# Four layers of attention, forward and backward: packed scores in layer 3, more transposes by DMA, and edits around them

## The chip, the core and the metric

The kernel runs on one core of a Trainium2 chip. The core has four compute engines with an instruction stream each: TensorE (PE, matmuls and transposes; its weight loads are listed as PEld), VectorE (DVE), ScalarE (ACT) and GpSimd (POOL). SyncE (SP) issues the DMAs, which run on 16 DMA engines. The metric is the device time of one execution in microseconds (us), and less is better.

## What is computed

Four residual layers over x of 2048 rows and 640 columns with 32 heads of 20: A, B, A, B, and then the gradients with respect to x and the four weights. The kernel numbers the layers 0 to 3: 0 and 2 are of kind A, 1 and 3 of kind B.

```python
def _A_ref(x, wqkv, wo):                    # linear attention
    ...
    phi = lambda t: jnp.where(t > 0, t + 1, jnp.exp(t)) + 1e-6
    pq, pk = phi(q), phi(k)
    kv = jnp.einsum("bhsd,bhse->bhde", pk, v)
    z = jnp.einsum("bhsd->bhd", pk)
    num = jnp.einsum("bhqd,bhde->bhqe", pq, kv)
    den = jnp.einsum("bhqd,bhd->bhq", pq, z)[..., None] + 1e-6
    ...
def _B_ref(x, wqkv, wo):                    # sliding window of 256
    ...
    scores = jnp.einsum("bhqd,bhkd->bhqk", q, k) * (Dh ** -0.5)
    mask = (idx[:, None] - idx[None, :] >= 0) & (idx[:, None] - idx[None, :] < W)
    p = _softmax(jnp.where(mask[None, None], scores, -1e9), axis=-1)
    o = jnp.einsum("bhqk,bhkd->bhqd", p, v)
    ...
x = x + _A_ref(_layernorm(x), A_wqkv, A_wo)
x = x + _B_ref(_layernorm(x), B_wqkv, B_wo)
x = x + _A_ref(_layernorm(x), A_wqkv, A_wo)
x = x + _B_ref(_layernorm(x), B_wqkv, B_wo)
_out, _vjp = jax.vjp(_f, A_x, A_wqkv, A_wo, B_wqkv, B_wo)
```

With tiles of 128 rows, a tile of queries meets three tiles of keys in a B layer: the first is half masked by the window (a key k counts for a query q of the tile if k > q), the middle one is full, and the last one is half masked by causality (k <= q).

## The kernel before

Rows are worked in 16 tiles of 128, heads in 8 groups of four. The order on PE, DVE, ACT and POOL is the order in which the program issues instructions. That order is written out by hand: the table PLACES (L41) holds due times, in slots, for the pieces of a tile's or a chunk's work, and `slots` (L737) sorts the pieces into the steps of the loop that carries the stage. SP's DMAs are all on one queue and start in the order of issue.

The stages follow each other. The forward of layer 0 is first. Then come 128 steps of layer 1, in which layer 0's rear and layer 2's front also run, and 128 steps of layer 3 with layer 2's rear. Next is the backward of layer 3, called a core: 8 chunks of two query tiles, 32 steps a chunk. The backward of linear layer 2 and the core of layer 1 follow. Last are the backward of layer 0 and the weight gradients, whose matmuls fill what PE has left (`fill`, L1298).

A forward step (`run`, L334) takes one query tile and one group. `f_scores` (L361) issues up to 12 matmuls: for each of the three key tiles one for each of four heads, which lie on four row groups of PE. Their output sT is one PSUM tile, with one buffer (L301). One exp on ACT (L376) turns all its columns, 128 for each key tile and head, into eT, which comes from a pool of five (L250). Then the due pieces of the plan are issued. After them `f_masks` (L379) zeroes the halves on POOL with two selects (L382 the diagonal, L386 the first key tile), and `b_pv` (L211) multiplies the eT of two steps before with the values, for each head and key tile. A backward core needs Wo transposed; for layer 3 a transposing DMA loads it near the end of the forward (L322, `turned`, L148).

A core step (`core_step`, L631) makes scores s and the products dp for a pair of heads, exp of s on ACT (L653), and ds = dp times e on DVE (L656). It transposes the ds of four steps before, either on PE with a copy by ACT or DVE (L676, L681, L683) or, where `by_dma` (L623) says so, with a transposing DMA that is issued as soon as ds is made. The table `bd` chooses these steps from step 64 on, `xx` shifts the copies between ACT and DVE, and warming transposes (`warm`, L168) are added where PE has little to do. The products (`core_acc`, L689) come `lag` = 7 steps behind the scores. Slabs of q, k and v are loaded a quarter of a chunk ahead.

`plan_before` (L743) prepares the gradient of the attention output for a chunk: g times Wo, the product with o summed over each head (`fold`, `split`, on POOL), and its transposes (`flip8`). For layer 1's first chunk it runs ahead of the core, inside the last slots of layer 2's backward (L1265 to L1267). `plan_linear` (L916) is the backward of a linear layer, in 8 slots a tile. Its `part` (L938) makes the gradient dqa: PE's product times fd, the derivative of phi, which is min(phi - 1e-6, 1) (L957 to L960).

Of the kernel before, what the change touches and what calls it, by code (L numbers as in the profile page):

```python
# [11 lines left out]
ALU = mybir.AluOpType  # L12
# [5 lines left out]
H = 32  # L18
DH = 20
HP = 32  # L20
T = 2048
TT = T // P
DT = D // P
# [18 lines left out]
    f1=[0.1, 1.7, 2.5, 6.6, 9.6, 12, 13.2, 14.1, 14.5, 14.6, 14.5, 16.1],  # L42
    f2=[-27.5, -23.6, -21.5, -20.6, -19.5, -17.9, -16.5, -15.1, -13.5, -7.8, -6.9, -5.5, -4.7, -3.8, -2.9, 11, 12, 13, 14, 17.6, 22.4, 23.3, 24, 25.1, 26.4, 27.3],
    f3=[-35.7, -30, -26.5, -25, -24, -23.8, -22.5, -18, -16.4, -14, -12.1, -7.4, -6.8, -6, -4.9, -3.5, -1.7, 11.3, 12.4, 13.4],
    bf=[2.1, 3.1, 5.7, 15.4, 18.3, 6.2, 7.8, 10, 14.7, 29.2],
    bh=[13.1, 14.5, 15.5, 17.1, 17.5, 18, 20.5, 21.2, 25.7, 28.3, 30, 35, 19.1, 20, 21.8, 22.5, 23.3, 24.6, 25.2, 27.5, 30.5, 31.7, 33, 35, 41, 43, 2.2, 8.3, 9.5, 12, 18.9, 32],
    l2=[-12.1, -3.2, 0.6, 0.7, 2.3, 2.7, 4.7, 5.6, 6.5, 7, 5, 8, 8.3, 11.5, 11.8, 14, 14.6, 15.4, 16, 17.7, 19.4],
    n1=[10, 0.8, 3.3, 3.5, 3.8, 7, 3.6, 4.2, 5.5, 6.6, 8],
    xx=[1, 0, 0, 0, 0, 0, 0, 1, 1, 0, 1, 0, 0, 1, 0, 0, 0, 1, 0, 0, 0, 0, 1, 0, 0, 0, 0, 0, 0, 0, 1, 0],
    bd=[0, 0, 1, 0, 0, 0, 1, 0, 0, 0, 0, 0, 0, 0, 1, 0, 0, 0, 1, 0, 0, 0, 1, 0, 0, 0, 1, 0, 0, 0, 1, 0])  # L50


class Kern:
    def __init__(self, ctx, tc, x0, A_w, A_wo, B_w, B_wo, grad, outs):
        self.ctx, self.tc = ctx, tc
        self.nc = nc = tc.nc
        self.W = dict(A=A_w, B=B_w)
        self.Wo = dict(A=A_wo, B=B_wo)
        self.grad = grad
# [36 lines left out]
        self.r = [const.tile([P, TT, H], F32, name=f"r{l}") for l in range(4)]  # L96
        self.mz = {l: const.tile([KB, 6, KA], BF, name=f"mz{l}") for l in (0, 2)}
        self.mzT = {l: const.tile([KA, 6, KB], BF, name=f"mzT{l}") for l in (0, 2)}
        self.dmz = const.tile([KB, 6, KA], BF, name="dmz")
        self.dmzT = const.tile([KA, 6, KB], BF, name="dmzT")  # L100
        self.macc = const.tile([KB, 6, KA], F32, name="macc")
# [109 lines left out]
    def b_pv(self, st, l, t, g, e, nb, rings, o):  # L211
# [4 lines left out]
            st.first = None  # L216
        for hh in range(4):
            for i in range(nb):
                ins = self.mm(st.ops[:, 4 * q + hh, :], e[:, hh, i * P:(i + 1) * P],
                              rings[i]["s"][:, 2, 4 * g + hh, 0:HA], st.first is None, i == nb - 1)  # L220
                if st.first is None:
                    st.first = ins
                else:
                    self.after(ins, st.first)
# [10 lines left out]
    def forward(self, st):  # L235
# [11 lines left out]
        st.sm = self.pool(keep, "fm", 4, side="right")  # L247
        st.fa = self.pool(keep, "fa", 3, side="right")
        st.xm = self.pool(keep, "xm", 5, side="right")
        st.fpe = self.pool(keep, "pe", 5, side="right")  # L250
        wo = self.pool(keep, "wo", 1, side="right")
        rings = {i: self.pool(keep if i in (0, 3, 4) else early, f"ring{i}", 1, side="right") for i in (0, 3, 4, 1, 2)}
        st.fb = self.pool(early, "fb", 3, side="right")
# [64 lines left out]
        def begin_slabs():  # L318
            early.close()
            self.core_slabs(3, st.core)  # L320
            self.core_buffers(st, st.core)
        plan += [(END - 32, begin_core), (END - 31, lambda: self.turned(st.core.WoT, "B")), (END - 6, begin_slabs)]  # L322
        first_ = {}

        def before(a):
# [8 lines left out]
        def run(n):  # L334
            u, fs = None, slots[n]
            if B1 <= n < B1 + G * TT:
                if n == B1:
                    for f in fs:
                        f()
                    fs = []  # L340
                u = self.f_scores(st, *divmod(n - B1, G), X[1])
            elif B3 <= n < END:
                u = self.f_scores(st, *divmod(n - B3, G), X[3])
            for f in fs:
                f()
# [15 lines left out]
    def f_scores(self, st, t, g, X):  # L361
# [5 lines left out]
        rings = [st.ring[(k0 + i) % len(st.ring)] for i in range(nb)]  # L367
        qT = st.ring[t % len(st.ring)]["T"]
        s = st.pS.tile([P, 4, 512], F32, name="sT")
        for i in range(nb):  # L370
            for hh in range(4):
                r0 = HP * hh
                self.mm(s[:, hh, i * P:(i + 1) * P], rings[i]["T"][r0:r0 + HP, 1, g, :], qT[r0:r0 + HP, 0, g, :],
                        True, True, (r0, 0))
        e = st.fpe.tile([P, 4, 3 * P], BF, name="eT")
        nc.scalar.activation(e[:, :, 0:nb * P], s[:, :, 0:nb * P], ACT.Exp)  # L376
        return t, g, e, nb, rings, X[t]["ob"]

    def f_masks(self, t, g, e, nb, rings, o):  # L379
        nc = self.nc  # L380
        dg = e[:, :, (nb - 1) * P:nb * P]
        nc.gpsimd.affine_select(out=dg, in_=dg, compare_op=ALU.is_ge, fill=0.0, base=0,  # L382
                                pattern=[[0, 4], [1, P]], channel_multiplier=-1)
        if nb == 3:
            fr = e[:, :, 0:P]
            nc.gpsimd.affine_select(out=fr, in_=fr, compare_op=ALU.is_ge, fill=0.0, base=-1,  # L386
                                    pattern=[[0, 4], [-1, P]], channel_multiplier=1)

    def plan_ln(self, st, l, t, x, src, key, pool):

# [349 lines left out]
            out[int(at)].append(fn)  # L740
        return [(lambda fs=fs: [f() for f in fs]) if fs else None for fs in out]

    def plan_before(self, st, l, c, B, at=(PLACES["bf"][:5], PLACES["bf"][5:]), l0=0):  # L743

        nc = self.nc
        r = self.r[l]
# [6 lines left out]
        for i, (f0, p0, p1, sp, f8) in enumerate(at):  # L753
# [12 lines left out]
            def fold(i=i, t=t):  # L766
                R = B.ring[t % 4]
                pr = x["pr", i] = B.sf.tile([P, H, DH], F32, name="prod")
                nc.gpsimd.tensor_tensor(out=pr, in0=R["ds"][:, :, 0:DH], in1=self.heads(x["o"][:, i, :]), op=ALU.mult)
                for m in (DH // 2, DH // 4):  # L770
                    nc.gpsimd.tensor_tensor(out=pr[:, :, 0:m], in0=pr[:, :, 0:m], in1=pr[:, :, m:2 * m], op=ALU.add)

            def split(i=i, t=t):
                R = B.ring[t % 4]
                m = DH // 4
                ds, pr = R["ds"], x["pr", i][:, :, 0:m]
                nc.gpsimd.tensor_scalar(out=ds[:, :, DH:DH + m], in0=pr, scalar1=-1.0, scalar2=None, op0=ALU.mult)
                nc.gpsimd.tensor_tensor(out=ds[:, :, DH + m:DH + 2 * m], in0=pr, in1=ds[:, :, DH:DH + m], op=ALU.add)

            def flip8(t=t):  # L780
                R = B.ring[t % 4]
# [134 lines left out]
    def plan_linear(self, st, lp, l, t, X, WT, g_out):  # L916
# [21 lines left out]
        def part(nm, c):  # L938
# [15 lines left out]
            if nm == "pk":  # L954
                nc.scalar.copy(dst, ps[:, 0:CW])  # L955
            else:
                f = lp.le.tile([P, CW], F32, name="fd")  # L957
                nc.vector.tensor_scalar(out=f, in0=src("pq" if nm == "dn" else "pk")[:, c * CW:(c + 1) * CW], scalar1=-EPS, scalar2=1.0,
                                        op0=ALU.add, op1=ALU.min)
                nc.vector.tensor_tensor(out=dst, in0=ps[:, 0:CW], in1=f, op=ALU.mult)  # L960

        def turn_q():
# [248 lines left out]
    def passes(self):  # L1211
# [6 lines left out]
        with ExitStack() as rest:  # L1218
# [45 lines left out]
                self.core_slabs(1, B)  # L1264
            b0 = base + 8 * (TT - 1) + PLACES["n1"][0]  # L1265
            plan.append((b0, begin))
            plan += [(b0 + a, f) for a, f, *_ in self.plan_before(st, 1, 0, B, (PLACES["n1"][1:6], PLACES["n1"][6:11]), -10)]  # L1267
            for f in self.slots(plan, int(max(a for a, _ in plan)) + 1):
                if f is not None:
                    f()  # L1270
# [2 lines left out]
            st.ps = st.ps2  # L1273

            self.core_buffers(st, B)
            left1 = self.core(st, 1, self.gs[0], B, [])
            for f in left1[:8]:
                if f is not None:
                    f()
# [8 lines left out]
            W.ps = self.pool(rest, "wp", 2, bass.MemoryType.PSUM, "right")  # L1288
            wl = self.pool(rest, "wl", 2)
            W.rhs = self.pool(rest, "wq", 2)  # L1290
            wo = self.pool(rest, "wo", 3)
            st.ex = self.pool(psl, "ex", 1)
            W.lhs, W.tight = [wl, wl], True
            W.out = lambda: wo.tile([P, 240], BF, name="wr")
# [24 lines left out]
            with ExitStack() as es, ExitStack() as le:  # L1319
# [11 lines left out]
                for f in self.slots(plan, int(max(a for a, *_ in plan)) + 1):  # L1331
                    if f is not None:
                        f()
                    fill(0.6)
            wl4 = self.pool(rest, "wl", 2)
            W.lhs += [wl4, wl4, wl, wl3]
            W.tight = False
# [61 lines left out]
```

## Time and profile before

| what | us |
|---|---|
| median of three runs (2276.66 to 2277.54) | 2276.91 |
| the profiled execution | 2281.01 |
| its span, first to last instruction | 2279.3 |
| layer 3 forward, 431 to 695 us: PE / DVE / ACT / POOL busy of 264 | 238 / 173 / 194 / 159 |
| core of layer 3, 695 to 1110: of 415 | 386 / 325 / 322 / 281 |
| layer 2 backward, 1184 to 1306: of 122 | 106 / 100 / 73 / 43 |
| core of layer 1, 1322 to 1746: of 424 | 395 / 332 / 329 / 288 |
| weight gradients alone, 2036 to 2280: of 244 | 240 / 19 / 11 / 0 |

In the lines of the profile, times in groups are a mean in ns or a sum in us; a line of a timeline has its start, its duration, the engine, the line of the code, the operation with the tiles it writes and reads, and in brackets how long the engine had stood idle and what ended that. A line of the windows view has a stretch, its length, the busy time of PE, PEld, DVE, ACT and POOL with counts, the granted clock of TensorE (1.00 is full speed), the DMA engines' mean busy share and GB/s.

### The profile page before, as it was taken

The numbers are of one execution on the slowest core, as the hardware profiler recorded it, in microseconds if no ns is written. First come the engines' busy times: TensorE is split into PE (matmuls) and PEld (weight loads), VectorE is DVE, ScalarE is ACT, GpSimd is POOL, SyncE is SP. The second block draws the span as 40 slices with busy tenths as digits, with TensorE's granted clock in tenths as the row PEclk, the third lists the DMA queues.
The fourth block names the chain that finished last, engine by engine and source line by source line (L and its number), as shares of the span: only waits on it lengthen the run. The fifth ranks groups of instructions, "written<-read, shape, count | busy, mean of one in ns | idle before, by whom it ended". The sixth has DMA issues, their size and how long they took to land. (4 is left out here: it accounts for less than half of the span.)

```text
span 2279.3 us, 77671 instructions
## 1 busy us (share of the span) xinstructions
PE 2096.7 (92%) x32468; PEld 1711.2 (75%) x32468; DVE 1453.8 (64%) x2980; ACT 1365.5 (60%) x2125; POOL 1092.1 (48%) x1892
## 2 busy tenths in 40 slices
PE   7889998899989999999878889999998898999999
PEld 5667776577767877777757768777777697889999
DVE  6778885777734788888748858888877244520000
ACT  5467887377766878878736668788876243430000
POOL 2046665166665577777533456777775312220000
PEclk9899999999989999999989999999999999999999
DMA  7488875698888577776488743777764999875753
GB/s 253 141 232 229 225 222 148 162 226 213 215 223 219 144 162 186 184 181 170 116 285 238 197 114 88 176 183 181 181 168 116 290 279 279 245 211 156 181 147 89
DMA packets 666992, 436.20 MB, mean 191 GB/s; under 512 B 406928, under 2 KB 643472, under 8 KB 666256
## 3 DMA queue, kind: packets, MB, share of 16 engines
q1 hardware_dynamic: 666640, 431.24, 71.4%
q8 instruction: 254, 4.16, 0.8%
q14 instruction: 98, 0.80, 0.1%
HBM read 213.09 MB, written 149.82 MB: 159 GB/s over the span
## 5 line engine op out<-in xcount | busy, mean ns | idle before, releaser
L656 DVE TENSOR_TENSOR ds<-dp,e 128x768 bf16<-128x768 f32 (+2 forms) x512 | 464.1, 906 | 159.9 <-PE s L136 62.4
L653 ACT ACTIVATE e<-s 128x768 bf16<-128x768 f32 (+2 forms) x512 | 396.0, 773 | 152.1 <-PE s L136 127.2
L376 ACT ACTIVATE eT<-sT 128x1536 bf16<-128x1536 f32 (+2 forms) x256 | 350.8, 1370 | 134.7 <-PE sT L136 133.3
L136 PE MATMUL wg<-rhs,lhs 128*128 128x240 bf16 (+1 forms) x3840 | 372.5, 256 | 6.2 <-DMA lhs<-o 6.2
L136 PEld LDWEIGHTS <-lhs 128*128 128x128 bf16 x3840 | 338.6, 98 | 22.2 <-DMA lhs<-o 6.9
L665 POOL TENSOR_SCALAR_AFFINE_SELECT e<-e 128x256 bf16<-128x256 bf16 x512 | 207.2, 406 | 262.6 <-ACT e L653 250.1
L136 PEld LDWEIGHTS <-dqT 128*128 128x128 bf16 x1920 | 175.9, 98 | 66.7 <-issue 12.3
L382 POOL TENSOR_SCALAR_AFFINE_SELECT eT<-eT 128x512 bf16<-128x512 bf16 x256 | 162.2, 635 | 112.6 <-ACT eT L376 111.6
L136 PE MATMUL acc<-slabqs,ds 128*128 128x20 bf16 x2880 | 210.1, 172 | 2.0 <-ACT dq L735 0.5
L676 PE MATMUL flip<-ident,ds 128*128 128x128 bf16 x2376 | 206.6, 221 | 5.2 <-ACT dsT L681 4.3
L136 PE MATMUL acc<-ds,e 128*128 128x20 bf16 x2880 | 208.2, 171 | 0.6 <-issue 0.6
L136 PE MATMUL dp<-slabvT,dT 32*128 32x384 bf16 (+2 forms) x1024 | 167.7, 321 | 39.6 <-DVE ds L656 35.2
L136 PEld LDWEIGHTS <-ds 128*128 128x128 bf16 x2880 | 188.1, 96 | 11.7 <-issue 3.5
L1083 DVE CAST wr<-wg 128x240 bf16<-128x240 f32 (+1 forms) x72 | 27.3, 379 | 265.2 <-PE wg L136 256.1
L669 POOL TENSOR_SCALAR_AFFINE_SELECT e<-e 128x256 bf16<-128x256 bf16 x448 | 196.0, 437 | 0.0
L1081 ACT CAST wr<-wg 128x240 bf16<-128x240 f32 (+1 forms) x48 | 16.1, 336 | 275.7 <-PE wg L136 268.7
L676 PEld LDWEIGHTS <-ds 128*128 128x128 bf16 x2376 | 144.0, 98 | 48.8 <-issue 46.5
L136 PEld LDWEIGHTS <-e 128*128 128x128 bf16 x2880 | 170.2, 96 | 12.4 <-issue 4.0
L136 PE MATMUL dense<-WB,hnT 128*128 128x320 bf16 x960 | 168.5, 308 | 2.8 <-DVE o L450 1.5
L136 PE MATMUL s<-slabkT,slabqT 32*128 32x384 bf16 (+2 forms) x1024 | 167.9, 324 | 3.1 <-ACT e L653 2.4
L1001 POOL TENSOR_TENSOR dh<-dh,lg 128x640 f32<-128x640 f32 x32 | 48.6, 1519 | 237.6 <-DVE s L998 233.4
L136 PE MATMUL dense<-WTA,dqT 128*128 128x320 bf16 x960 | 154.2, 300 | 6.3 <-ACT dqa L955 5.6
(168 smaller groups left out, 4631.4 us busy)
## 6 DMA issues: line engine op xcount, KB each, us to landing
rhs<-dqkv SPq DMA_DIRECT2D x64, 480.0 KB, 5.2
s<-s SPq DMA_DIRECT2D x32, 768.0 KB, 3.8
T<-T SPq DMA_DIRECT2D x32, 768.0 KB, 4.0
dqkv<-dq SPq DMA_DIRECT2D x16, 960.0 KB, 5.6
dqkv<-dqa SPq DMA_DIRECT2D x32, 480.0 KB, 4.3
slabkT<-T SPq DMA_DIRECT2D x56, 256.0 KB, 5.1
slabvT<-T SPq DMA_DIRECT2D x56, 256.0 KB, 3.2
slabks<-s SPq DMA_DIRECT2D x56, 256.0 KB, 3.5
```

The costliest lines, as they stand in the source:

```text
L136: return self.nc.tensor.matmul(out, lhsT=lhsT, rhs=rhs, start=start, stop=stop, skip_group_check=True, **kw)
L376: nc.scalar.activation(e[:, :, 0:nb * P], s[:, :, 0:nb * P], ACT.Exp)
L382: nc.gpsimd.affine_select(out=dg, in_=dg, compare_op=ALU.is_ge, fill=0.0, base=0, pattern=[[0, 4], [1, P]], channel_multiplier=-1)
L653: nc.scalar.activation(u.e[:, :, 0:u.cw], s[:, :, 0:u.cw], ACT.Exp)
L656: nc.vector.tensor_tensor(out=d.ds[:, :, 0:d.cw], in0=d.dp[:, :, 0:d.cw], in1=d.e[:, :, 0:d.cw], op=ALU.mult)
L665: nc.gpsimd.affine_select(out=dg, in_=dg, compare_op=ALU.is_ge, fill=0.0, base=0, pattern=[[0, 2], [-1, P]], channel_multiplier=1)
L669: nc.gpsimd.affine_select(out=fr, in_=fr, compare_op=ALU.is_ge, fill=0.0, base=-1, pattern=[[0, 2], [1, P]], channel_multiplier=-1)
L676: nc.tensor.transpose(ps[:, 3 * j + i, :], f.ds[:, j, i * P:(i + 1) * P], self.ident)
L1001: nc.gpsimd.tensor_tensor(out=x["dh"], in0=x["dh"], in1=L["g"][:, i, :], op=ALU.add)
L1081: nc.scalar.copy(o[:, 0:w], ps[:, 0:w])
L1083: nc.vector.tensor_copy(o[:, 0:w], ps[:, 0:w])
```

## The change

In layer 3, for query tiles with three key tiles (`self.halves`), the scores of one head take 320 columns instead of 384. Columns 0 to 127 hold the middle key tile, 128 to 255 the last one. Columns 256 to 319 hold the first key tile for the first 64 queries. Keys 64 to 127 of the first tile for queries 64 to 127 are written over the part of the last tile that causality masks: partitions 64 to 127 of columns 128 to 191. Exp runs over 320 columns; POOL copies the quarter out to columns 320 to 383 with a select that also masks it, then masks the diagonal and the first tile. The eT tiles become five fixed ones, so that the zeros in their columns 320 to 383 of partitions 0 to 63 are written once, at the start of layer 3; `b_pv` reads the blocks in their new places.

Beside it: Wo of layer 3's core is transposed on PE from the copy that the forward holds (`turn_wo`); 13 instead of 7 of 32 core steps transpose ds by DMA, and other due times and shares of the tables move; fd is written in bfloat16 by an instruction with a second tensor operand, a broadcast column of ones; for layer 1's first chunk the first tile's `fold` and `split` run on DVE (`quick`), and the pieces due from 20 on run inside the core's first steps; the weight gradients' output pool has five buffers instead of three, and `fill` puts 0.8 us of them in a slot of layer 0's backward instead of 0.6.

```diff
-    bf=[2.1, 3.1, 5.7, 15.4, 18.3, 6.2, 7.8, 10, 14.7, 29.2],
...
-    n1=[10, 0.8, 3.3, 3.5, 3.8, 7, 3.6, 4.2, 5.5, 6.6, 8],
-    xx=[1, 0, 0, 0, 0, 0, 0, 1, 1, 0, 1, 0, 0, 1, 0, 0, 0, 1, 0, 0, 0, 0, 1, 0, 0, 0, 0, 0, 0, 0, 1, 0],
-    bd=[0, 0, 1, 0, 0, 0, 1, 0, 0, 0, 0, 0, 0, 0, 1, 0, 0, 0, 1, 0, 0, 0, 1, 0, 0, 0, 1, 0, 0, 0, 1, 0])
+    bf=[2.1, 3.1, 5.2, 14.9, 17.9, 6.2, 7.8, 10, 14.6, 28.3],
...
+    n1=[9.7, 0.5, 3.3, 3.6, 5.3, 9, 3, 4.7, 5.4, 5.6, 24],
+    xx=[1, 1, 0, 0, 0, 0, 1, 1, 0, 0, 0, 0, 0, 1, 0, 0, 1, 0, 0, 0, 0, 0, 0, 1, 0, 0, 1, 0, 0, 0, 1, 0],
+    bd=[0, 0, 1, 0, 0, 0, 1, 0, 0, 0, 0, 0, 0, 1, 1, 0, 0, 1, 1, 0, 1, 0, 1, 0, 1, 0, 1, 1, 0, 1, 1, 0])
...
+        self.one = const.tile([P, 1], BF, name="one")
+        nc.gpsimd.memset(self.one, 1.0)
...
-                ins = self.mm(st.ops[:, 4 * q + hh, :], e[:, hh, i * P:(i + 1) * P],
+                b = (i + 2) % 3 if self.halves and nb == 3 else i
+                ins = self.mm(st.ops[:, 4 * q + hh, :], e[:, hh, b * P:(b + 1) * P],
...
-        st.fpe = self.pool(keep, "pe", 5, side="right")
+        fpe = self.pool(keep, "pe", 1, side="right")
+        st.fe, self.halves = [fpe.tile([P, 4, 3 * P], BF, name=f"eT{i}") for i in range(5)], False
...
-        plan += [(END - 32, begin_core), (END - 31, lambda: self.turned(st.core.WoT, "B")), (END - 6, begin_slabs)]
+        plan += [(END - 32, begin_core), (END - 6, begin_slabs)]
+
+        def turn_wo(j):
+            tp = st.ps.tile([P, 8, P], BF, name="flip", tag="m")
+            for k in range(DT):
+                nc.tensor.transpose(tp[:, k, :], WoB[:, k, j * P:(j + 1) * P], self.ident)
+            nc.vector.tensor_copy(st.core.WoT[:, j, :], tp[:, 0:DT, :].rearrange("p a b -> p (a b)"))
+        plan += [(END - 31.5 + 2 * j, lambda j=j: turn_wo(j)) for j in range(DT)]
...
+                if n == B3:
+                    self.halves = True
+                    for e in st.fe:
+                        nc.gpsimd.memset(e[0:HALFP, :, 5 * HALFP:6 * HALFP], 0.0)
...
+        if self.halves and nb == 3:
+            for c0, i, q0, n, k0 in ((0, 1, 0, P, 0), (P, 2, 0, P, 0), (2 * P, 0, 0, HALFP, 0), (P, 0, HALFP, HALFP, HALFP)):
+                for hh in range(4):
+                    score(hh, c0, rings[i], q0, n, k0)
+            w = 5 * HALFP
...
+        nc.scalar.activation(e[:, :, 0:w], s[:, :, 0:w], ACT.Exp)
...
+        if self.halves and nb == 3:
+            keep(e[HALFP:P, :, 5 * HALFP:6 * HALFP], e[HALFP:P, :, P:P + HALFP], HALFP, False)
+            dg = e[:, :, P:2 * P]
+            keep(dg, dg, P, True)
+            fr = e[:, :, 2 * P:2 * P + HALFP]
+            keep(fr, fr, HALFP, False)
...
+                eng = nc.vector if quick and i == 0 else nc.gpsimd
...
-                f = lp.le.tile([P, CW], F32, name="fd")
-                nc.vector.tensor_scalar(out=f, in0=src("pq" if nm == "dn" else "pk")[:, c * CW:(c + 1) * CW], scalar1=-EPS, scalar2=1.0,
-                                        op0=ALU.add, op1=ALU.min)
+                f = lp.le.tile([P, CW], BF, name="fd")
+                nc.vector.scalar_tensor_tensor(out=f, in0=src("pq" if nm == "dn" else "pk")[:, c * CW:(c + 1) * CW], scalar=-EPS,
+                                               in1=self.one.to_broadcast([P, CW]), op0=ALU.add, op1=ALU.min)
...
-            plan += [(b0 + a, f) for a, f, *_ in self.plan_before(st, 1, 0, B, (PLACES["n1"][1:6], PLACES["n1"][6:11]), -10)]
+            fs = self.plan_before(st, 1, 0, B, (PLACES["n1"][1:6], PLACES["n1"][6:11]), -10, True)
+            plan += [(b0 + a, f) for a, f, *_ in fs if a < 20]
+            hooks = self.slots([(a - 20, f) for a, f, *_ in fs if a >= 20], 8)
...
-            left1 = self.core(st, 1, self.gs[0], B, [])
+            left1 = self.core(st, 1, self.gs[0], B, [f or (lambda: None) for f in hooks])
...
-            wo = self.pool(rest, "wo", 3)
+            wo = self.pool(rest, "wo", 5)
...
-                    fill(0.6)
+                    fill(0.8)
```

More of the change, by code (lines that the diff above doesn't have):

```diff
@@ L20 @@
 HP = 32
+HALFP = P // 2
 T = 2048
@@ L44 @@
     f3=[-35.7, -30, -26.5, -25, -24, -23.8, -22.5, -18, -16.4, -14, -12.1, -7.4, -6.8, -6, -4.9, -3.5, -1.7, 11.3, 12.4, 13.4],
-    bf=[2.1, 3.1, 5.7, 15.4, 18.3, 6.2, 7.8, 10, 14.7, 29.2],
-    bh=[13.1, 14.5, 15.5, 17.1, 17.5, 18, 20.5, 21.2, 25.7, 28.3, 30, 35, 19.1, 20, 21.8, 22.5, 23.3, 24.6, 25.2, 27.5, 30.5, 31.7, 33, 35, 41, 43, 2.2, 8.3, 9.5, 12, 18.9, 32],
-    l2=[-12.1, -3.2, 0.6, 0.7, 2.3, 2.7, 4.7, 5.6, 6.5, 7, 5, 8, 8.3, 11.5, 11.8, 14, 14.6, 15.4, 16, 17.7, 19.4],
-    n1=[10, 0.8, 3.3, 3.5, 3.8, 7, 3.6, 4.2, 5.5, 6.6, 8],
-    xx=[1, 0, 0, 0, 0, 0, 0, 1, 1, 0, 1, 0, 0, 1, 0, 0, 0, 1, 0, 0, 0, 0, 1, 0, 0, 0, 0, 0, 0, 0, 1, 0],
-    bd=[0, 0, 1, 0, 0, 0, 1, 0, 0, 0, 0, 0, 0, 0, 1, 0, 0, 0, 1, 0, 0, 0, 1, 0, 0, 0, 1, 0, 0, 0, 1, 0])
+    bf=[2.1, 3.1, 5.2, 14.9, 17.9, 6.2, 7.8, 10, 14.6, 28.3],
+    bh=[13.1, 14.5, 15.5, 17.1, 17.5, 18, 20, 21.2, 25.7, 28.3, 30, 36, 19.1, 20.1, 21.8, 22.5, 23.3, 24.6, 25.2, 27.5, 30.5, 31.7, 33, 35, 41.5, 43, 2.2, 8.3, 9.5, 12, 18.9, 34.5],
+    l2=[-10.4, -1.3, 0.6, 1.2, 1.9, 3.2, 4.6, 6.2, 7, 7.5, 5, 8, 8.3, 10.2, 11.8, 14, 14.4, 15.4, 16, 16.2, 18.7],
+    n1=[9.7, 0.5, 3.3, 3.6, 5.3, 9, 3, 4.7, 5.4, 5.6, 24],
+    xx=[1, 1, 0, 0, 0, 0, 1, 1, 0, 0, 0, 0, 0, 1, 0, 0, 1, 0, 0, 0, 0, 0, 0, 1, 0, 0, 1, 0, 0, 0, 1, 0],
+    bd=[0, 0, 1, 0, 0, 0, 1, 0, 0, 0, 0, 0, 0, 1, 1, 0, 0, 1, 1, 0, 1, 0, 1, 0, 1, 0, 1, 1, 0, 1, 1, 0])
 class Kern:
@@ L369, in f_scores, with score @@
         s = st.pS.tile([P, 4, 512], F32, name="sT")
[L370 to L376, printed above, removed]
+        e = st.fe[0]
+        st.fe.append(st.fe.pop(0))
+        def score(hh, c0, k, q0, n, k0=0):
+            r0 = HP * hh
+            self.mm(s[k0:P, hh, c0:c0 + n], k["T"][r0:r0 + HP, 1, g, k0:P], qT[r0:r0 + HP, q0:q0 + n], True, True, (r0, k0))
+        qT = qT[:, 0, g, :]
+        if self.halves and nb == 3:
[3 more added lines that the diff above has]
+            w = 5 * HALFP
+        else:
+            for i in range(nb):
+                for hh in range(4):
+                    score(hh, i * P, rings[i], 0, P)
+            w = nb * P
+        nc.scalar.activation(e[:, :, 0:w], s[:, :, 0:w], ACT.Exp)
         return t, g, e, nb, rings, X[t]["ob"]
@@ L380, in f_masks, with keep @@
         nc = self.nc
[L381 to L387, printed above, removed]
+        def keep(out, in_, w, up):
+            s = 1 if up else -1
+            nc.gpsimd.affine_select(out=out, in_=in_, compare_op=ALU.is_ge, fill=0.0, base=0 if up else -1,
+                                    pattern=[[0, 4], [s, w]], channel_multiplier=-s)
+        if self.halves and nb == 3:
[4 more added lines that the diff above has]
+            keep(fr, fr, HALFP, False)
+        else:
+            dg = e[:, :, (nb - 1) * P:nb * P]
+            keep(dg, dg, P, True)
+            if nb == 3:
+                fr = e[:, :, 0:P]
+                keep(fr, fr, P, False)
     def plan_ln(self, st, l, t, x, src, key, pool):
@@ L741, in slots, with plan_before @@
         return [(lambda fs=fs: [f() for f in fs]) if fs else None for fs in out]
-    def plan_before(self, st, l, c, B, at=(PLACES["bf"][:5], PLACES["bf"][5:]), l0=0):
+    def plan_before(self, st, l, c, B, at=(PLACES["bf"][:5], PLACES["bf"][5:]), l0=0, quick=False):
         nc = self.nc
@@ L768, in fold @@
                 pr = x["pr", i] = B.sf.tile([P, H, DH], F32, name="prod")
-                nc.gpsimd.tensor_tensor(out=pr, in0=R["ds"][:, :, 0:DH], in1=self.heads(x["o"][:, i, :]), op=ALU.mult)
+                eng = nc.vector if quick and i == 0 else nc.gpsimd
+                eng.tensor_tensor(out=pr, in0=R["ds"][:, :, 0:DH], in1=self.heads(x["o"][:, i, :]), op=ALU.mult)
                 for m in (DH // 2, DH // 4):
-                    nc.gpsimd.tensor_tensor(out=pr[:, :, 0:m], in0=pr[:, :, 0:m], in1=pr[:, :, m:2 * m], op=ALU.add)
+                    eng.tensor_tensor(out=pr[:, :, 0:m], in0=pr[:, :, 0:m], in1=pr[:, :, m:2 * m], op=ALU.add)
             def split(i=i, t=t):
@@ L776, in split @@
                 ds, pr = R["ds"], x["pr", i][:, :, 0:m]
-                nc.gpsimd.tensor_scalar(out=ds[:, :, DH:DH + m], in0=pr, scalar1=-1.0, scalar2=None, op0=ALU.mult)
-                nc.gpsimd.tensor_tensor(out=ds[:, :, DH + m:DH + 2 * m], in0=pr, in1=ds[:, :, DH:DH + m], op=ALU.add)
+                eng = nc.vector if quick and i == 0 else nc.gpsimd
+                eng.tensor_scalar(out=ds[:, :, DH:DH + m], in0=pr, scalar1=-1.0, scalar2=None, op0=ALU.mult)
+                eng.tensor_tensor(out=ds[:, :, DH + m:DH + 2 * m], in0=pr, in1=ds[:, :, DH:DH + m], op=ALU.add)
             def flip8(t=t):
```

## The prediction

> **What bounds the kernel now.** First the busy shares, then the waits of TensorE (PE), then the stages where it waits.
>
> ```profile
> PE 2096.7 (92%) x32468; PEld 1711.2 (75%) x32468; DVE 1453.8 (64%) x2980; ACT 1365.5 (60%) x2125; POOL 1092.1 (48%) x1892
> ```
>
> PE is the bound as an average, so a part of the change pays only if it takes instructions off PE or ends a wait of PE. The windows view gives the stages: layer 3 forward (431 to 695 us) has PE busy 238 of 264, its backward core (695 to 1110) 386 of 415, layer 2 backward (1184 to 1306) 106 of 122, the second core (1322 to 1746) 395 of 424; from 1840 on it is full. I take the edits stage by stage.
>
> **A. Packed scores, layer 3.** The timeline of ScalarE (ACT) and PE in one middle query tile:
>
> ```profile
> 559.95 1.45 ACT L376 ACTIVATE eT<-sT 128x1536 bf16<-128x1536 f32 x1 [0.53 <-PE sT L136]
> 561.93 1.45 ACT L376 ACTIVATE eT<-sT 128x1536 bf16<-128x1536 f32 x1 [0.53 <-PE sT L136]
> ...
> 561.45 0.29 PE L136 MATMUL sT<-T,T 32*128 32x128 bf16 x8 [0.28 <-ACT eT L376]
> ...
> 563.48 0.29 PE L136 MATMUL sT<-T,T 32*128 32x128 bf16 x8
> 563.60 0.22 PE L136 MATMUL sT<-T 32*128 32x128 bf16 x4
> 563.76 0.85 PE L136 MATMUL dense<-WB,hnT 128*128 128x320 bf16 x5
> ```
>
> The score tile has one buffer: exp waits for the scores, the next scores for exp. That loop is 1.45 + 0.53 = 1.98 us, and the exps begin 1.98 apart in over half of the steps; eight take 16.47 us, not 15.84, because in the others PE is late. So two bounds lie close together. The exps of 512 and 1536 columns last 593 and 1450 ns, 0.84 ns a column; 1280 columns give 1236, 214 ns less in 112 steps: 24 us at most. PE is busy 15.43 of 16.40 us in such a tile, so only about 1 us of it can go. And the packing needs 16 score matmuls instead of 12. Twelve take 0.28 us from their start to the next group's (563.48 to 563.76), 23 ns each; four more cost 0 (if columns set the time: 1536 before and after) to 0.09 us. Eight steps: up to 0.74 us of PE a tile. Left are 0.3 to 1.0 us in some 11 steady tiles; in the last three, where exps are 1.98 apart and PE has less to do, I count 0.15 x 24 steps = 3.6. **A = -8** (ends -15 and +10: nothing gained and 112 x 0.09 paid). GpSimd (POOL) gets three selects for two: two of 634 ns become 634 and two of 256 columns at 406 (the core's row of that size), +0.18 us a step. It is busy 10.2 of 16.4 us and the products with the values run two steps behind, so that is covered; without the cover it would be 112 x 0.18 = 20 us. The fixed buffers rotate over five as the pool did; five small memsets fall where POOL is busy 1.1 of 29 us.
>
> **B. Wo of layer 3 turned on PE.** Now it is one transposing load on SyncE's queue (SP), ahead of the transposes of the keys:
>
> ```profile
> 635.00 5.04 SPq L106 DMA_TRANSPOSE T<-s  x1
> ...
> 642.02 0.40 PE L136 MATMUL sT<-T,T 32*128 32x128 bf16 x8 [3.32 <-DMA T<-s]
> ```
>
> The 3.32 us go, and some 0.7 us of half clock behind them (these score groups take 0.40, not 0.29). Added: 25 transposes at 55 ns (six of L676 take 0.33) and five copies of 0.48 on a VectorE (DVE) that waits in this stage: 1.4 to 2. **B = -2** (-5 to +1.5). Next late is exp.
>
> **C. More transposes by DMA in the backward cores.** The instruction order has 156 of the score gradients' transposes on SP instead of 84: six more in each of 12 chunks. Each takes six PE transposes (0.33 us) and one copy away (0.55 us on DVE or 0.79 on ACT; DVE loses 56, ACT 16). The warming transposes stay 906. PE: 432 x 55 ns = 23.8 us. Rows of one chunk and of four:
>
> ```profile
> 904.90:961.30 56.40, 53.15 (x1018) 42.76 (x1018) 47.16 (x71) 45.79 (x76) 42.60 (x83) 1.00 0.79 182
> ...
> PE dp L136 <- DVE ds L656: 10.5, 24, 0.9
> PE flip L676 <- ACT dsT L681: 1.5, 8, 0.2
> PE acc L136 <- DMA dsT<-ds: 1.2, 2, 0.9
> ```
>
> PE is busy 94%, so its work goes nearly one to one. It also waits 2.6 us a chunk for DVE, part of which should go. Against it stands DMA. A transpose is 768 packets of 256 B, 29 ns each in the packet records: 1.39 us of all 16 engines. Six more raise the chunk's 44.4 us (0.79 of 56.4) to 52.8, while the chunk would shrink to 54.4: 0.97. A share of 1.05 appears at 1780 to 1800 us, so it fits, with nothing to spare. SP issues six more of 1.22 us, 7.3 a chunk. Behind a transpose waiting for DVE's ds stand slab loads (needed eight steps on) and dqT; a result is used four steps on, about 7 us, and lands 2.8 us after its issue (median). **C = -22** (-40 to 0).
>
> **D. The factor fd of the linear layers.** DVE, POOL and PE in one tile of layer 2:
>
> ```profile
> 1284.77 0.32 DVE L958 TENSOR_SCALAR fd<-lpqk 128x320 f32<-128x320 bf16 x1
> 1285.59 0.94 DVE L958 TENSOR_SCALAR fd<-lpqk 128x320 f32<-128x320 bf16 x1
> 1287.04 1.43 DVE L958 TENSOR_SCALAR fd<-lpqk 128x320 f32<-128x320 bf16 x1
> ...
> 1286.75 1.54 POOL L1008 TENSOR_TENSOR lgn<-dh,lna 128x640 bf16<-128x640 f32 x1 [0.40 <-ACT lna L1007]
> ...
> 1289.12 0.32 PE L136 MATMUL dense<-dmz,pkT 120*128 120x40 bf16 x4 [0.95 <-DVE dqa L960]
> ```
>
> fd takes 0.32 us alone, and until POOL's add ends where one runs. PE then waits 0.93 to 0.95 in nearly every tile (13 waits, 12.0 us). The new form reads two SBUF tensors. Here rule and row part. The Trainium skill, "GPSIMD Engine Reference", section "8. Key points", says that DVE contends with POOL in its two-port mode *or with two SBUF inputs*: by it the stalls stay, each instruction is 0.17 longer (0.49, as DVE's 320-column rows), and PE loses about 5 us more. The row is lna (L863, two SBUF inputs): 825 ns alone, 1040 with POOL running, a quarter more and not until POOL's end. By it fd is 0.49 to 0.62, four are 2.0 to 2.5 us instead of 3.0, and the late one is up to 0.8 earlier. I follow the row: 13 x 0.7, **D = -9** (-12 to +5). In layer 0 the same edit is worth nothing: PE is full there.
>
> **E. Into the second core.**
>
> ```profile
> 1318.96 0.63 PE L785 MATMUL flip<-ident,ds 128*128 128x128 bf16 x8 [4.03 <-POOL ds L778]
> 1321.79 0.29 PE L136 MATMUL s<-slabkT,slabqT 32*128 32x128 bf16 x2 [1.97 <-ACT e L653]
> ```
>
> POOL makes prod, its sums and ds for two tiles in a row, 4.1 us each (1.35 + 1.41 + 0.68 + 0.57). The change gives the first to DVE and puts the second's turn into the core's fourth step: the 4.03 go, the 1.97 (exp with other ACT work ahead) perhaps not. The first score matmuls are cold behind the stall, about 1 us. **E = -5** (-9 to 0).
>
> **F. The end.** More weight-gradient work a slot (0.8 for 0.6) moves full PE time about; five output buffers instead of three free copies. A PE wait of 5.58 us at 1884 (a store of dqa queued behind large loads) may move, go or double: **F = -1** (-6 to +6). The moved due times I cost at 0: no instruction is added and the nearest work on each engine is the same.
>
> **Sum.** -8 -2 -22 -9 -5 -1 = -47. The profiled execution took 2281.0 (span 2279.3); 2281.0 - 47 = 2234. The median shown is 4.1 lower, so 2276.9 - 47 = **2230**.
>
> **Rivals.**
> 1. *The transposes come late (slower).* The core's order leaves PE standing at acc until dsT has landed. The six such long waits of before are 0.82, 0.87, 1.87, 0.64, 1.81 and 1.88, mean 1.3. If each of the 72 new ones waits that long, 94 us are added: 2324. It decides from 0.65 us each (47 / 72). For it: the 0.97 share. Against: only six long waits among 84.
> 2. *DMA eats C.* Queueing returns what PE saves: 2230 + 22 = 2252. For it: the same share; against: SP's own idle time.
> 3. *The packing does not do what it says and fd stalls on.* PE sets layer 3's step and the rule is right in D: A = +10, D = +5, 2230 + 18 + 14 = 2262.
> 4. *Freed DVE pays too.* The 2.6 us a chunk go as well, 12 x 2 = 24: 2206.
>
> **How the numbers follow.** Forecast 0.46 (own range 2214 to 2246), rival 2 0.20, rival 4 0.13, rival 1 0.11, rival 3 0.08, no change 0.02. The range 2202 to 2264 leaves out rival 1 and little else. Within 0.2% (4.6 us) a measurement of this kernel cannot tell a change. Faster is the sum without rival 1, no change and a part of the low shares: 0.86; same 0.02; slower 0.12.
>
> **What would show it.** A: exps of about 1240 ns, some 15.8 us a tile instead of 16.47, hardly any wait of scores for exp. B: no wait at 640. C: a chunk of about 54.5 us, a DMA share near 0.95, waits of acc for dsT of a few us in all. D: fd near 0.5 everywhere, 7.0 us a tile instead of 7.69. E: no 4 us wait near 1315. The forecast falls if acc waits for DMA by tens of us, or if score groups of 16 take 0.4 us and a tile stays at 16.4.

## The result, and the profile after

The changed kernel takes 2253.2 us (median of four runs, 2247.6 to 2256.1) against 2277.2; the ratio is 0.9889 with a 95% interval of 0.9867 to 0.9910. The forecast was 2230 with a range of 2202 to 2264: the sign and the range were right, but only half of the 47 us came. The shares of the whole span tell little:

```profile
PE 2094.3 (93%) x32509; PEld 1705.5 (76%) x32509; DVE 1456.7 (65%) x2934; ACT 1337.5 (59%) x2109; POOL 1118.9 (50%) x2005
...
q1 hardware_dynamic: 721008, 444.58, 78.3%
```

PE is as busy as before (2096.7 us), although 432 transposes went: something else was added to it. The DMA queue's share rose from 71.4% to 78.3%. Cut at the same instructions, the two profiled executions (spans 2279.3 and 2254.4) differ so:

| stretch | before | after | change | predicted |
|---|---|---|---|---|
| up to layer 3's first exp | 431.4 | 429.9 | -1.5 | 0 |
| layer 3 forward, to the core's first exp (A, B) | 263.8 | 263.5 | -0.3 | -10 |
| core of layer 3, first to last exp (C) | 437.3 | 427.4 | -9.9 | -11 |
| to layer 2's first fd | 51.5 | 50.2 | -1.3 | 0 |
| layer 2, first to last fd (D) | 120.4 | 115.8 | -4.6 | -9 |
| to the next core's first exp (E) | 17.0 | 13.9 | -3.1 | -5 |
| core of layer 1 (C) | 436.7 | 433.5 | -3.2 | -11 |
| to the end (F) | 521.2 | 520.2 | -1.0 | -1 |

The surprise is the forward: the edit that names the change gained nothing. The timelines of PE and ACT in a middle tile show why:

```profile
512.48 0.45 PE L139 MATMUL ops<-s,eT 128*128 128x21 bf16 x12
512.86 0.23 PE L139 MATMUL sT<-T,T 32*128 32x128 bf16 x4
512.92 0.22 PE L139 MATMUL sT<-T 32*128 32x128 bf16 x4
512.98 0.35 PE L139 MATMUL sT<-T,T 32*128 32x64 bf16 x8
513.26 0.45 PE L139 MATMUL dense<-WB,hnT 128*128 128x320 bf16 x2
...
507.44 1.24 ACT L406 ACTIVATE eT<-sT 128x1280 bf16<-128x1280 f32 x1 [0.66 <-PE sT L139]
509.33 1.24 ACT L406 ACTIVATE eT<-sT 128x1280 bf16<-128x1280 f32 x1 [0.66 <-PE sT L139]
```

Exp takes 1.24 us as worked out. But the score group lasts 0.40 us to the next group's start (512.86 to 513.26), not 0.28. The group is a part of the loop of exp and scores, so exps whose loop sets the pace are 1.89 us apart, only 0.09 less than before. And in most steps PE no longer waits for exp (5.8 us in the stage, 15.8 before). Windows rows of one such tile before and after, and of the whole stage after, have the bill:

```profile
508.60:525.05 16.45, 15.48 (x285) 11.98 (x283) 12.35 (x33) 12.84 (x11) 10.21 (x17) 1.00 0.83 216
507.44:523.97 16.53, 16.49 (x317) 12.59 (x315) 12.48 (x33) 11.46 (x11) 12.08 (x25) 1.00 0.92 215
429.90:693.40 263.50, 250.70 (x4660) 191.70 (x4658) 176.06 (x453) 173.50 (x170) 185.88 (x382) 0.98 0.85 215
```

In the tile PE is busy for 16.49 of 16.53 us, where it had 1.0 us free before. In the stage it is busy 250.7 us, 12 more than the 238.3 of before, and ACT 20 less. The bound went from the loop of exp and scores to PE, at the same length.

In layer 2 the stall of fd is still there. This is DVE, GpSimd and PE in one tile:

```profile
1223.97 1.70 POOL L1044 TENSOR_TENSOR dh<-dh,lg 128x640 f32<-128x640 f32 x1 [3.71 <-DVE s L1041]
1225.97 1.54 POOL L1051 TENSOR_TENSOR lgn<-dh,lna 128x640 bf16<-128x640 f32 x1 [0.30 <-ACT lna L1050]
1224.91 1.11 DVE L1001 SCALAR_TENSOR_TENSOR fd<-lpqk,one 128x320 bf16<-128x320 bf16 x1
1226.53 1.32 DVE L1001 SCALAR_TENSOR_TENSOR fd<-lpqk,one 128x320 bf16<-128x320 bf16 x1
1228.36 0.48 DVE L1001 SCALAR_TENSOR_TENSOR fd<-lpqk,one 128x320 bf16<-128x320 bf16 x1
...
1228.50 0.32 PE L139 MATMUL dense<-dmz,pkT 120*128 120x40 bf16 x4 [0.45 <-DVE dqa L1003]
```

Two of a tile's four fd last 1.1 and 1.3 us. Both begin while GpSimd runs an add and end 0.35 us after it. So it is with all 28 long fd of the layer (over 0.6 us), and none of the 36 short ones begins in an add. In the kernel before it is the same 28, and all but one end 0.18 us after the add. The tile is shorter all the same (7.25 us, 7.69 before), and PE waits 0.45 where it waited 0.95. Since fd stalls on, something else must have helped; the experiments on layer 2 separate the two.

### The profile page after: what moved, and what is told of

Its sections match the earlier page's. It is cut to its first block, busy times and chain, and to the rows that moved or that the text cites. A ratio compares the mean times of both kernels' runs of the same rounds, so it can differ in the third digit from the quotient of the medians.

```text
span 2254.4 us, 78069 instructions
## 1 busy us (share of the span) xinstructions
PE 2094.3 (93%) x32509; PEld 1705.5 (76%) x32509; DVE 1456.7 (65%) x2934; ACT 1337.5 (59%) x2109; POOL 1118.9 (50%) x2005
## 3 DMA queue, kind: packets, MB, share of 16 engines
q1 hardware_dynamic: 721008, 444.58, 78.3%
## 5 line engine op out<-in xcount | busy, mean ns | idle before, releaser
L406 ACT ACTIVATE eT<-sT 128x1280 bf16<-128x1280 f32 (+3 forms) x256 | 327.1, 1278 | 150.0 <-PE sT L139 138.3
L415 POOL TENSOR_SCALAR_AFFINE_SELECT eT<-eT 128x512 bf16<-128x512 bf16 (+2 forms) x592 | 319.2, 560 | 88.8 <-ACT eT L406 57.1
L139 PEld LDWEIGHTS <-ds 128*128 128x128 bf16 x2880 | 188.1, 96 | 11.8 <-issue 3.5
L1044 POOL TENSOR_TENSOR dh<-dh,lg 128x640 f32<-128x640 f32 x32 | 51.5, 1610 | 256.2 <-DVE s L1041 246.8
L717 PE MATMUL flip<-ident,ds 128*128 128x128 bf16 x1944 | 169.8, 221 | 3.3 <-DVE ds L804 1.2
L139 PE MATMUL dense<-WTA,dqT 128*128 128x320 bf16 x960 | 162.6, 301 | 1.2 <-DMA dqT<-dqa 0.9
L139 PE MATMUL acc<-slabks,dsT 128*128 128x20 bf16 x2880 | 147.1, 171 | 13.0 <-DMA dsT<-ds 13.0
```

The source lines that it names most:

```text
L139: return self.nc.tensor.matmul(out, lhsT=lhsT, rhs=rhs, start=start, stop=stop, skip_group_check=True, **kw)
L406: nc.scalar.activation(e[:, :, 0:w], s[:, :, 0:w], ACT.Exp)
L415: nc.gpsimd.affine_select(out=out, in_=in_, compare_op=ALU.is_ge, fill=0.0, base=0 if up else -1, pattern=[[0, 4], [s, w]], channel_multip ...
L717: nc.tensor.transpose(ps[:, 3 * j + i, :], f.ds[:, j, i * P:(i + 1) * P], self.ident)
L1044: nc.gpsimd.tensor_tensor(out=x["dh"], in0=x["dh"], in1=L["g"][:, i, :], op=ALU.add)
```

## Experiments

The kernel before, measured beside the experiments, spread over 2269 to 2284 us: its fastest run had a mean granted clock of 0.982, its slowest one of 0.976. Differences of some us between kernels are therefore read in the stages of their profiles, and the ratios give the whole.

### What the packing costs

**The packing alone.** The kernel before with `f_scores`, `f_masks`, `b_pv` and the eT tiles of the change, nothing else.

> The kernel before with only the packing of layer 3's scores (f_scores, f_masks, b_pv, the five fixed eT tiles, the zeros). Theory 1, PE took the bound over: score groups take 0.40 us instead of 0.28, the exps are 1236 ns, but layer 3's forward (first exp to first exp of the core, 263.8 us before) stays within 2 us of 263.8, and the kernel within 3 us of 2277. Theory 2, another edit spoiled the packing: the forward falls by about 8 us and the kernel to about 2269.

2278.1 us, ratio 1.000 (0.9984 to 1.0015); layer 3's forward 264.5 us. The packing gains nothing by itself either, so no other edit spoiled it.

**Which part of the added work: the count, or the tile's shape?** Two kernels change only the list of score matmuls. The first lets the quarter take all 128 keys, and so overwrites a part of the last tile's scores; the second leaves the quarter out. Both keep the rest of the step.

```diff
-            for c0, i, q0, n, k0 in (..., (2 * P, 0, 0, HALFP, 0), (P, 0, HALFP, HALFP, HALFP)):
+            for c0, i, q0, n, k0 in (..., (2 * P, 0, 0, HALFP, 0), (P, 0, HALFP, HALFP, 0)):    # quarter wide
+            for c0, i, q0, n, k0 in (..., (2 * P, 0, 0, HALFP, 0)):                             # no quarter
```

> The changed kernel, in which the quarter's four matmuls take all 128 keys (they overwrite a part of the last key tile's scores, so a part of layer 3 is computed from other keys): 16 matmuls as before, but all on tiles of 32 rows and 128 columns. Theory 1, the change of PE's tile shape costs (the quarter starts 125 ns after the round ahead of it, other rounds 57): the group takes about 0.33 us and a steady tile falls from 16.5 to about 16.0 us, 5 to 6 us in all. Theory 2, the number of matmuls costs: the group stays at 0.40 and the tile at 16.5.

> The changed kernel without the quarter's four matmuls (keys 64 to 127 of the first tile are left out for queries 64 to 127): 12 matmuls, exp over 320 columns. Both theories that blame the quarter: the group back at 0.28 us, a steady tile at 15.5 to 15.8 us, layer 3's forward about 10 us shorter than the changed kernel's. If POOL's chain or DVE sets the step instead, the tile stays at 16.5.

The group in the middle of the stage, in PE's timeline of the first and then of the second (32\*128 are the rows and columns of PE's tile, 32x64 the moving operand; a row with x8 holds two rounds of four):

```profile
512.69 0.23 PE L139 MATMUL sT<-T,T 32*128 32x128 bf16 x4
512.76 0.22 PE L139 MATMUL sT<-T 32*128 32x128 bf16 x4
512.81 0.23 PE L139 MATMUL sT<-T,T 32*128 32x64 bf16 x8
512.97 0.85 PE L139 MATMUL dense<-WoB,obT 128*128 128x320 bf16 x5
```

```profile
512.47 0.23 PE L139 MATMUL sT<-T,T 32*128 32x128 bf16 x4
512.53 0.22 PE L139 MATMUL sT<-T 32*128 32x128 bf16 x4
512.59 0.20 PE L139 MATMUL sT<-T,T 32*128 32x64 bf16 x4
512.72 0.85 PE L139 MATMUL dense<-WoB,obT 128*128 128x320 bf16 x5
```

Sixteen matmuls on tiles of one shape take 0.28 us (512.69 to 512.97), twelve 0.25. The count costs 0.03 us a step; the quarter's own tile, 32 rows by 64 columns, costs 0.12. The single records say where: in the changed kernel the quarter starts 126 ns after the round ahead of it, the wide quarter with the same moving operand 28 ns after it. That is 0.10 of the 0.12; the rest lies between the quarter and the next group. The wide quarter differs in the tile's columns (128 for 64) and in where they begin (0 for 64), and these runs don't separate the two. Writing over the last tile's columns is ruled out as the cause, for the wide quarter does it too. A steady tile takes 16.5 us with the quarter, 16.0 with it wide, 15.75 without; the forward 263.5, 257.7 and 252.9; the kernels 0.9865 (0.9841 to 0.9888) and 0.9860 (0.9837 to 0.9882) of before.

The Trainium skill has the rule, in "TensorEngine Tiling (Array Packing)", section "Key Properties": changing the tiling mode drains the engine. These runs put 0.12 us on it here. That the array drains is the page's word; the runs show the delay and that it goes with the narrow tile. All eight groups of a query tile measure so in the changed kernel (0.40 to 0.41 us), and seven of the eight with the quarter wide (0.28). The query tile gives back 0.5 us of eight times 0.12; where the rest goes is not worked out. As wholes, the two kernels do not differ, though their forwards do by 5 us.

**Packing where PE has time.** From the trace of before, PE waits for exp at the scores of groups 0, 1 and 2, that is behind the exps of groups 7, 0 and 1. This kernel packs only those, and all groups of the last three tiles. The buffers then hold both layouts in turn, so the quarter's select covers all partitions and the zeros are not written ahead. It also has the old fd (below).

```diff
+    def packed(self, t, g, nb):
+        return self.halves and nb == 3 and (t >= 13 or g in (7, 0, 1))
```

> The changed kernel with fd in its old form, and with the scores packed only where TensorE waited for exp before (groups 7, 0 and 1 of a tile, and all groups of tiles 13 to 15); other steps as before. Theory 1 (a packed group costs PE 0.13 us and saves exp 0.21): a steady tile falls from 16.5 to about 16.1 us, layer 3's forward to some 258 us, and with layer 2 at 7.0 a tile the kernel comes to about 2243, 10 below the changed one. Theory 2, the loop of exp and scores and PE's order shift the wait into the next step: the tile stays at 16.4 to 16.5 and the kernel near 2248.

A tile takes 16.2 us, the forward 259.2. The mechanism holds in the stage, and the gain is 4 us instead of 0. The kernel takes 2248.0, ratio 0.9877 (0.9856 to 0.9897), not the 2243 of theory 1. The changed kernel with the old fd, its partner for the packing alone, takes 2247.9 (below). So the mix is better in its stage and not shown faster as a whole.

**Wo turned by DMA again.** The changed kernel with line 322 of before in place of `turn_wo`.

> The changed kernel with Wo of layer 3 turned by the transposing DMA as before, not on PE. Theory 1, the stall of 2.2 to 3.3 us was traded for an equal amount of PE work (25 transposes in a stage where PE is the bound): layer 3's forward stays within 1 us of 263.5. Theory 2, as the prediction had it: the stall comes back at tile 12 and the forward grows by 2 us or more.

Layer 3's forward is 264.3 us, 0.8 more, with a wait of 1.9 us for T in it; 2255.1 us, ratio 0.9893 (0.9868 to 0.9918). The stall was traded for about as much PE work. In the profiles of the kernel before and of its variants the same stall measured 2.2 to 3.3 us, and with `turn_wo` instead of the DMA the forward is 0.8 us shorter here and 1.0 against the packing alone, so B's value is 0 to 1 us.

### The cores: transposes by DMA

**Only the tables.** The kernel before with the change's `bd`, `xx`, `bf` and `bh`.

> The kernel before with only the core's tables of the change (bd, xx, bf, bh): 156 transposes by DMA instead of 84. Theory 1, the tables made the cores' gain alone: the 16 chunks lose 13 us together as in the changed kernel (874.0 to 860.9), the kernel about 2263, with a DMA share of 1.0 and more in the chunks. Theory 2, the gain is limited by something else that the change brought along: 20 us and more.

The two cores take 862 us together (874.0 before, 860.9 in the changed kernel), the kernel 0.9919 (0.9902 to 0.9935). In the four profiles with 7 of 32 steps by DMA the cores take 868 to 874 us, in the nine with 13 they take 856 to 862: 12 us less in the mean. The tables made the cores' gain, and by the stages it is half of the whole. The edits of `bd`, `xx` and the due times in them were not separated.

**More of it.** The changed kernel with 16 ones in `bd` (10, 15 and 28 added).

> The changed kernel with 16 instead of 13 of 32 steps transposed by DMA (36 more in all). If PE's work sets the core and DMA has room, chunks 2 to 7 of both cores fall by another 5 to 6 us (18 fewer flips a chunk at 41 ns, 12 chunks: 9 us less of PE busy, a third of it lost to waits). If DMA is at its limit (its share is already 1.0 to 1.06 in a chunk), they grow, and the waits of acc for dsT rise from 13 us to 30 and more.

2268.3 us, ratio 0.9964 (0.9948 to 0.9980): slower than with 13. For chunks 2 to 7 of both cores, summed up from the traces:

| by DMA, of 32 | length | PE busy | waits for DVE's ds | waits for dsT by DMA |
|---|---|---|---|---|
| 7 (before) | 683.9 | 632.6 | 34.0 | 8.7 |
| 13 (after) | 671.3 | 614.7 | 36.7 | 12.8 |
| 16 | 685.0 | 611.8 | 40.2 | 27.6 |

PE's waits in chunks 2 to 7 of the first core, after the change and then with 16:

```profile
PE dp L139 <- DVE ds L697: 17.0, 42, 0.9
PE acc L139 <- DMA dsT<-ds: 5.0, 5, 2.3
```

```profile
PE dp L139 <- DVE ds L697: 19.6, 46, 0.9
PE acc L139 <- DMA dsT<-ds: 15.5, 13, 2.2
```

And a chunk of the changed kernel in the windows view:

```profile
944.00:999.40 55.40, 51.35 (x985) 41.23 (x983) 45.64 (x67) 45.55 (x77) 43.38 (x84) 1.00 0.96 212
```

From 7 to 13 PE's busy time falls by 17.9 us and its idle time grows by 5.3: net 12.6. From 13 to 16 the busy time falls by only 3 and the waits for dsT double. That is not for want of work taken away. With 16, eight of the twelve chunks hold a stretch of 3.4 us in which the granted clock is one half; with 13 there are four such stretches, with 7 three. One of them, after a wait for dsT, and the chunk that it lies in beside the next one:

```profile
1555.88 0.31 PE L139 MATMUL acc<-slabks,dsT 128*128 128x20 bf16 x6 [1.96 <-DMA dsT<-ds]
1556.40:1559.80 3.40, 3.40 (x36) 1.99 (x33) 2.23 (x3) 2.60 (x6) 0.77 (x2) 0.50 1.36 216
...
1523.20:1581.40 58.20, 52.08 (x969) 40.65 (x967) 44.00 (x64) 44.59 (x74) 42.58 (x83) 0.97 1.05 210
1581.40:1636.60 55.20, 50.53 (x970) 40.22 (x969) 43.78 (x64) 44.49 (x74) 42.76 (x83) 1.00 1.02 217
```

At full clock a chunk with 16 takes 55.2 to 56.2 us, one with 13 takes 54.7 to 56.3, one with 7 takes 55.8 to 57.3. So 16 loses time in the chunks with a stretch at half clock, nearly all of which also hold a late transpose. An estimate from these counts: a stretch loses half of 3.41 us, so 13.7 us are lost with 16, 6.8 with 13 and 5.1 with 7. At full clock PE's work falls by 19.6 us from 7 to 13 and by 9.8 from 13 to 16, both 45 ns a transpose. Against the 9.8 stand 14.8 us more of waits for dsT, 3.5 for ds and 6.8 of lost clock.

The half clock follows the late transposes. In chunks 2 to 7 of all fourteen profiles there are 44 such stretches. 39 begin within 5 us after a wait of 1.4 us or more for dsT, and 39 of the 48 such waits have one behind them; of 95 shorter waits (0.3 to 1.4 us) five have. That is an order in time and not an experiment: no run takes the waits away and leaves the rest. The mean granted clock agrees: with 16 steps its median over the runs is 0.972, in the other kernels 0.976 to 0.979.

The DMA share of a chunk was 0.79 at most before and comes up to 1.10 now. A transpose lands 3.9 us after its issue (median of the middle chunks of the first core), not 2.8. With 16 steps the share rises no further (1.09 at most) and the landing takes 4.0. This speaks for DMA engines near the edge of what they carry; no run varies their load in another way.

### Layer 2: the form of fd and its due times

> The kernel before with only the new form of fd (two SBUF inputs, bfloat16). Theory 1, the form contends with GpSimd as before, so that it adds 0.17 us an instruction and takes no stall away: a tile of layer 2 stays at 7.7 us or grows to 8.1 (13 tiles: 0 to 5 us longer), PE's wait for dqa at 0.9 us or more. Theory 2, as the prediction had it: 7.0 us a tile, 9 us less.

> The kernel before with only the new due times of the linear backward (table l2). Theory 1, the due times made layer 2's gain: a tile falls from 7.7 us to 7.2 or less, some 6 us in layer 2, and fd keeps its stalls up to 1.4 us. Theory 2, the form of fd made it: the tile stays at 7.7.

> The changed kernel with fd in its old form. Theory 1, the new form only lengthens DVE, which is busy 13.7 of 14.5 us in two tiles of layer 2: the tile falls from 7.25 to about 7.0 us, 3 us in all. Theory 2, the form pays: the tile grows to 7.7, 6 us more.

The first has only lines 1000 to 1002 of the change and the column of ones, the second only its table `l2`, the third is the changed kernel with lines 957 to 959 of before.

| kernel | a tile of layer 2, us | first to last fd | ratio to before |
|---|---|---|---|
| before | 7.69 | 120.4 | 1 |
| new form alone | 7.9 | 123.6 | 1.0021 (1.0010 to 1.0032) |
| new due times alone | 7.0 | 111.8 | 0.9969 (0.9957 to 0.9981) |
| both (the change) | 7.25 | 115.8 | 0.9889 (0.9867 to 0.9910) |
| the change with the old form | 7.0 | 110.8 | 0.9880 (0.9861 to 0.9900) |

The due times gained 9 us in this stretch and the form gave 5 of them back. With the due times alone 2 of the 9 return on the way into the second core (from the last fd to its second chunk 60.1 us, 58.0 before), which fits the kernel as a whole (2268.4 us against 2275.1). DVE and PE with the due times alone:

```profile
1226.34 0.94 DVE L958 TENSOR_SCALAR fd<-lpqk 128x320 f32<-128x320 bf16 x1
1227.79 1.43 DVE L958 TENSOR_SCALAR fd<-lpqk 128x320 f32<-128x320 bf16 x1
...
1229.87 0.32 PE L136 MATMUL dense<-dmz,pkT 120*128 120x40 bf16 x4 [0.28 <-DVE dqa L960]
```

fd stalls as long as before. PE comes to the product that needs DVE's dqa later, with other matmuls in between, and waits 0.28 us instead of 0.95. With the new form each fd is 0.16 longer when alone, still long beside GpSimd (28 of 64 over 0.6 us, as many as before). DVE is then busy 13.7 of 14.5 us in two tiles, and PE 13.6 or less. The old form put back makes the tile 7.0 us.

### The entry into the second core, and the end

> The changed kernel with the entry into layer 1's core as before (fold and split of the first tile on GpSimd, nothing in the core's first steps, the old times n1). Theory 1, the stall only moved, from the turn of ds to the first scores behind a copy on ACT: from the last fd of layer 2 to the core's second chunk the time changes by less than 2 us. Theory 2, the new entry saves 5 us: it grows by 5.

From the last fd to the core's second chunk it takes 59.8 us with the old entry and 56.1 with the new: the new one saves 3.7 us, nearer to theory 2. The kernel takes 2257.7, ratio 0.9922 (0.9903 to 0.9940), whose interval still overlaps the changed kernel's. PE's lines with the old entry:

```profile
1301.03 1.03 PE L828 MATMUL flip<-ident,ds 128*128 128x128 bf16 x8 [5.26 <-POOL ds L821]
1303.16 0.29 PE L139 MATMUL s<-slabkT,slabqT 32*128 32x128 bf16 x2 [1.10 <-ACT dT L829]
```

and with the new one:

```profile
1300.35 0.23 PE L139 MATMUL s<-slabkT,slabqT 32*128 32x128 bf16 x2 [3.27 <-ACT dT L829]
...
1306.80 0.29 PE L139 MATMUL dp<-slabvT,dT 32*128 32x128 bf16 x2 [0.74 <-DVE ds L697]
```

The wait for GpSimd went, and most of it came back at the core's first scores, which now wait for a copy that stands on ACT behind layer 2's last lna; the core's first chunk is 1 to 2 us longer for the turn that moved into it.

> The changed kernel with 0.6 us of weight gradients a slot and three output buffers. Theory 1, PE is full there and only its order moves: from the last exp of layer 1's core to the end 520 us, within 3. Theory 2, the waits for stores and loads matter: 525 or more.

From the last exp of layer 1's core to the end: 523.2 us, against 520.2 in the changed kernel and 521.2 before; 2256.5 us, ratio 0.9917 (0.9896 to 0.9938). This is inside the spread of the same stretch in kernels that share the new tail (519.3 to 524.1). What the buffers and the fill are worth is not settled.

## Why the prediction was half right

**A, the packing: -8 predicted, 0 measured.** The view was right: two bounds lie close together, and "the packing needs 16 score matmuls instead of 12". The term that failed is its price, "four more cost 0 to 0.09 us": it was 0.12. Sixteen on tiles of one shape take 0.28 us like the twelve of before, so the end at 0 was right for the count, and the 0.12 belong to the narrow tile. I took the group's time as a number of matmuls. The lines of before already had the sign: rounds of scores follow each other after 0.06 us, but the dense matmul on the whole array starts 0.16 after the last round (563.60 to 563.76). Eight steps of 0.12 are 1.0 us a tile, all that PE had free. The longer group also stands inside the loop of exp and scores; the sum took it as PE's time alone. The first half of rival 3 came true, and so did the sign that the forecast named for its fall: groups of 0.40 us, and a tile that stays (16.45 before, 16.53 after). POOL's third select shows only in PE's waits for eT, 2.2 us in the stage against 1.1.

**B, Wo: -2 predicted, 0 to -1 measured.** The stall went and PE's added work took its place.

**C, the cores: -22 predicted, -13 measured.** The mechanism was right, two sizes were not. A transpose taken away freed 41 ns of PE's busy time (17.9 us over 432), not 55; with the half clock counted out it is some 45, an estimate, and why it is not 55 stays open. And 5.3 us went into waits, 4.1 of them for late transposes, on which one more stretch of half clock follows: the prediction priced the half clock in B and E, but not here. That is part of rival 2, and with 16 steps one sees rival 1's mechanism begin. Rival 4 fell: copies taken off DVE did not shorten PE's waits for ds, which grew by 2.7 us.

**D, fd: -9 predicted, -4.6 measured, for another reason.** Two steps failed. "I follow the row": lna with two SBUF inputs beside GpSimd's selects (0.4 and 1.0 us) was no model for fd beside its adds (1.5 to 1.7 us), behind whose end every long fd ends; the rule of the skill ("GPSIMD Engine Reference", section "8. Key points") was the better guide, and the form alone cost 0.2% of the kernel. And "the moved due times I cost at 0": they were the gain. An order that lets PE arrive later at the operand took most of the wait away, with no instruction added. That D came out as a gain at all is luck: the edit on which it was argued lost time, and one that stood beside it paid.

**E and F: -5 and -1 predicted.** E measured -1.9 to the second chunk against before, and -3.7 against the old entry with otherwise changed code. The 4.03 us behind GpSimd went, as forecast, but the first scores now wait 3.27 us for a copy on ACT, where they waited 1.97 before. F: within noise.

The terms fell short by 8, 1, 9, 4 and 3 us, 25 in all; the medians, 24 us apart instead of 47, lack 23.

## What to carry to other kernels

When a matmul on small tiles is split, price the change of the tile's shape, not the count of matmuls: here a second shape took 0.12 of a group's 0.40 us. Where two bounds are within a few per cent, spend the saving only in the steps where the first one binds, and look whether the whole follows the stage. When a transfer comes late, look at the clock behind the wait as well as at the wait. And a table of due times is an edit like any other: test it alone before you credit the instruction beside it.

## What the runs showed of the hardware

- A round of four score matmuls on tiles of 32 rows by 64 columns starts 126 ns after a round on tiles of 32 by 128. On tiles of 32 by 128, with the same moving operand, it starts after 28 ns. The group of 16 takes 0.40 us with the second shape and 0.28 without.
- fd on DVE takes 0.32 us in its old form and 0.48 with two SBUF inputs. Every fd of layer 2 that begins in one of GpSimd's adds ends just after the add: 0.18 us later in the old form (27 of 28), 0.35 in the new one (28 of 28), up to 1.5 and 1.3 us long. lna, also with two SBUF inputs, went only from 0.82 to 1.04 beside selects of 0.4 and 1.0.
- With 13 of 32 steps transposed by DMA the packets' time comes to 0.75 to 1.10 of the 16 engines in chunks 2 to 7 (0.53 to 0.79 with 7), and three steps more doubled PE's waits for them at the same share.
- After most waits of PE of 1.4 us or more for a transpose (39 of 48) a stretch of 3.41 us at half clock follows, and a chunk that holds one is some 3 us longer (58.2 against 55.2 us with 16 steps).
